# Attention chunks of 128 steps as two halves of 64 on quarters of TensorE, in a kernel with two dense layers

## The chip, the cores and the metric

The kernel runs on one core of a Trainium2 chip. The metric is the device time of one execution in microseconds (us), the median over runs. TensorE is called PE, VectorE DVE, ScalarE ACT, GpSimd POOL, and SyncE, whose queue issues all DMAs here, SP.

## What is computed

A gated linear attention (an mLSTM cell, with 4 batches, 8 heads, 768 steps and head size 40) is followed by two feed-forward layers of 3072 tokens x 320, with 2048 hidden units each.

```
for t in range(S):
    m_new = maximum(f[t] + m, i[t])
    f_stab, i_stab = exp(f[t] + m - m_new), exp(i[t] - m_new)
    C = f_stab * C + i_stab * outer(v[t], k[t])        # 40 x 40 state per head
    n = f_stab * n + i_stab * k[t]
    y[t] = sigmoid(o[t]) * (C @ q[t]) / maximum(abs(n @ q[t]), 1)
h = x @ w_in;  g = where(h >= 1, h, where(h <= -1, 0, (h + 1)**2 / 4));  x = g @ w_out
h = x @ w_in2; g = maximum(h, 0)**2;                   out = g @ w_out2
```

## The kernel before

**Attention.** The 768 steps of a batch are cut into 6 chunks of L = 128, which makes 24 chunks; they run step-major (the first chunk of each of the 4 batches, then the second ones). `attention` makes one chunk out of these steps on PE: `scores` (L618, 8 matmuls, one per head, on two 64-row halves of the array), `outer` (L653, 3 matmuls of 3 heads each, the chunk's contribution to the state), `read0` and `read1` (L690, 3 matmuls that read the state C of the previous chunk, and L694, 8 matmuls of weighted scores with v). All are fp32. The 128x128 decay matrix of each head comes from a scan along time on DVE (`decay`, L587, two of 512 elements for a chunk); its input is a row of gate factors that must stand on all 128 partitions. For the first 4 chunks PE spreads it (`spread`, L582), for the 20 others a DMA does (`fb`). `ab`, the decay from the chunk's start, is loaded for the 20 others too, and scales q (`q_in`, L639) and the old state (`update`, L667). `mask` (L673) keeps the blocks of the 3-head products that belong to one head. The ninth head is padding.

**Dense layers.** A chunk's 128 outputs are transposed (L767, or a DMA through DRAM), split into a high and a low half, and gathered in blocks of 3 chunks (layer one, 8 blocks) or 4 (layer two, 6 blocks). `dense` makes, for one block and one of 16 slices of hidden units, `mm1` (L828, 8 matmuls), an activation on ACT, DVE and POOL, and `mm2` (L888, 3 matmuls per chunk of the block). A weight slice arrives as float64 in a DMA of 704 KB (`wraw`) and is converted on ACT and DVE (L339 to L380) and split (L321, then L393, or for the slices of `PLO` on PE and ACT: `sub`, L428 and L429, and `put`).

**Order.** Nothing is issued as written: each step gets a rank (a due time plus the tables `MOVE` and `SHIFT_OF`), an engine and a cost, and `Plan.order` plays the list through and writes down each engine's order. Every engine then runs its own order strictly. Where the plan has nothing for PE, it puts idle matmuls of zeros (`idle`, L968, 400 of them), all in the first 63 us. Tiles come from pools with the numbers of buffers in `bufs`.

Of the kernel before, what the change touches and what calls it, by code (L numbers as in the profile page):

```python
# [13 lines left out]
U16 = mybir.dt.uint16  # L14
# [5 lines left out]
R = B * HP  # L20
L = 128
# [10 lines left out]
CST = 4 * L + 3 * E + 2  # L32

# [5 lines left out]
class Plan:  # L39
# [6 lines left out]
    TABLE = {"sig": "sigmoid", "a1": "exp", "a2": "exp", "a3": "exp"}  # L46
# [8 lines left out]
    def add(self, eng, rank, dur, fn, need=(), make=()):  # L55
# [5 lines left out]
        if self.group:  # L61
            kind, i = self.group
            rank += SHIFT_OF.get(kind, {}).get(fn.__name__, 0) + (MOVE[kind][i] if kind in MOVE else 0)
        self.tags.append(self.group)
        self.steps.append((eng, rank, fn, tuple(need), tuple(make)))

    def order(self):
# [49 lines left out]
        port, table = 0.0, None  # L117
        while len(out) < n:
# [41 lines left out]
def pool(n):  # L160
# [10 lines left out]
SPR = 4  # L171
# [6 lines left out]
EARLY = 1  # L178
QB = 1
GATE = -14  # L180
MOVE = {
# [8 lines left out]
}  # L190
SHIFT_OF = {
    "g": {"v1": -37.86, "v1f": 3.09, "v1i": 6.32, "a2": -19.57, "a3": 5.93, "p1": 92.77, "d1": 39.25,
        "tp": -0.65, "cp": 4.15, "a1": 24.16, "p2": 22.67, "v2": -89.15, "d2": -66.11},
    "w": {"load": 0.92, "a_move": 46.15, "v_clamp": 0.63, "a_tail": 26.69, "v_sign16": 0.71, "v_join": 0.16,
        "a_hi": 9.08, "v_lo": -1.71, "lo": -3.28, "sub": 40.36, "put": 19.14},
    "x": {"ld_qk": 5.06, "ld_vko": 0.42, "spread": 0.06, "decay": 0.65, "last": -81.57, "weigh": 1.85,
        "scores": -0.79, "v_in": -9.46, "sig": -40.49, "k_in": 4.18, "outer": -0.01, "update": -19.59,
        "read0": -0.49, "read1": -25.45, "norm_a": 0.11, "norm_b": -14.27, "norm_c": -9.8, "again": -32.29,
        "tr": 0.35, "hi": -27.45, "lo": -15.74, "ld_f": -3.57, "ld_q": 3.84, "ld_a": 33.49, "q_in": 9.92,
        "mask": 13.98, "turn": -23.51, "store": 14.75, "load": -1.24},  # L200
    "y": {"load": 0.18, "hi": -1.5, "lo": 54.98},
    "d": {"mm1": 0.62, "relu": 12.79, "square": 5.59, "gate": -1.83, "hi": 21.06, "lo": 6.71, "mm2": 3.97,
        "keep": 9.14, "evac": -16.97, "turn": -21.93, "store": -2.59},
}
# [17 lines left out]
def kernel(  # L222
# [14 lines left out]
        wraw=RAWB, wt=3, qk=2, vko=2, fb=1, qh=QB, ab=QB, d0=DB, d1=DB,  # L237
        ws=2, vt=2, qt=2, kt=2, sg=2, xn=2, rc=2, cx=1, C=5, xTh=XTB, xTl=XTB, pa=PAB, r=3, g0=3, g1=3, o=2, x2=2,
# [16 lines left out]
    csb = const.tile([128, CST], F32, name="csb")  # L255
# [282 lines left out]
    def attention(n, at, spr, early=0, bounce=False):  # L538
# [158 lines left out]
        def read0():  # L697
            read(0)
# [394 lines left out]
```

## Time and profile before

| | us |
|---|---|
| median of 3 runs (857.73 to 862.39) | 858.11 |
| the profiled execution | 861.52 |
| its span, first to last instruction | 859.7 |
| PE busy | 849.5 (99%) |
| DVE, ACT, POOL busy | 440.3, 449.7, 364.5 |
| DMA: 81.41 MB, the 16 engines' share | 33.2% |

Busy time of PE counts overlapping matmuls once, and a matmul's shown duration has its latency in it: what a step costs PE is read from start to start. An fp32 matmul of the program stands in the trace as two records.

### The profile page before, as it was taken

The numbers are of one execution on the slowest core, as the hardware profiler recorded it, in microseconds if no ns is written. First come the engines' busy times: TensorE is split into PE (matmuls) and PEld (weight loads), VectorE is DVE, ScalarE is ACT, GpSimd is POOL, SyncE is SP. The second block draws the span as 40 slices with busy tenths as digits, with TensorE's granted clock in tenths as the row PEclk, the third lists the DMA queues.
The fourth block names the chain that finished last, engine by engine and source line by source line (L and its number), as shares of the span: only waits on it lengthen the run. The fifth ranks groups of instructions, "written<-read, shape, count | busy, mean of one in ns | idle before, by whom it ended". The sixth has DMA issues, their size and how long they took to land.

```text
span 859.7 us, 14945 instructions
## 1 busy us (share of the span) xinstructions
PE 849.5 (99%) x5619; PEld 801.4 (93%) x5619; DVE 440.3 (51%) x758; ACT 449.7 (52%) x877; POOL 364.5 (42%) x349
## 2 busy tenths in 40 slices
PE   9998999999999999999999999999999999999998
PEld 8897999999999999999999999999999999999997
DVE  4998788987878734555224768721221111111111
ACT  5655566865545464444678866644333443533332
POOL 3221343032323435646565665645443533633332
PEclk9998899999999999999999999999999999999999
DMA  7767545455646533453231234101110100100000
GB/s 232 209 202 231 163 129 174 158 150 151 168 119 149 163 80 106 123 144 76 68 74 49 100 88 117 41 1 38 50 50 1 29 31 1 59 0 1 32 1 31
DMA packets 116957, 81.41 MB, mean 95 GB/s; under 512 B 57348, under 2 KB 105768, under 8 KB 116884
## 3 DMA queue, kind: packets, MB, share of 16 engines
q1 hardware_dynamic: 116884, 80.45, 33.2%
q8 instruction: 44, 0.72, 0.4%
q14 instruction: 29, 0.24, 0.1%
HBM read 69.90 MB, written 10.52 MB: 94 GB/s over the span
## 4 chain that ended last, share of the span: by engine, by line
PE 88%; DVE 4%; DMA 4%; ACT 2%; issue 1%; SPq 1%; POOL 0%; ACTq 0%; DVEq 0%; POOLq 0%
PE h L828 39%; PE acc L888 33%; PE v L888 5%; PE v L694 4%; DMA wraw<-in_wts_dram 2%; PE s L618 2%; PE v L690 2%; PE acc L968 1%; PE v L653 1%; DVE d L587 1%; DMA ab<-a 1%; DMA x<-xn 0%; DMA fb<-f 0%; DVE r L846 0%; DVE wt L380 0%
## 5 line engine op out<-in xcount | busy, mean ns | idle before, releaser
L860 POOL TENSOR_TENSOR xTh<-xTl,xTh 128x512 fp32r<-128x512 f32 x96 | 125.5, 1308 | 177.7 <-ACT xTh L321 177.7
L888 PE MATMUL acc<-w,g 128*128 128x320 f32 x1152 | 196.8, 313 | 0.7 <-ACT w L321 0.7
L848 DVE TENSOR_TENSOR xTl<-xTl,h 128x512 f32<-128x512 f32 x96 | 66.0, 687 | 233.3 <-ACT xTl L835 233.2
L888 PEld LDWEIGHTS acc<-w,g 128*128 128x128 f32 x1152 | 176.2, 188 | 2.5 <-ACT w L321 1.2
L828 PE MATMUL h<-xTh,w 128*128 128x384 f32 x640 | 177.9, 343 | 0.6 <-DVE r L846 0.4
L888 PE MATMUL acc<-w,xTh 128*128 128x320 f32 x864 | 143.3, 309 | 0.0
L888 PEld LDWEIGHTS acc<-w,xTh 128*128 128x128 f32 x864 | 134.6, 188 | 8.1
L828 PE MATMUL h<-qk,w 128*128 128x512 f32 x384 | 135.7, 394 | 0.0
L828 PE MATMUL h<-xTl,w 128*128 128x384 f32 x384 | 130.2, 339 | 0.0
L828 PEld LDWEIGHTS h<-xTh,w 128*128 128x128 f32 x640 | 118.1, 190 | 2.4 <-DVE r L846 0.9
L833 ACT ACTIVATE r<-h,half 128x384 f32<-128x384 f32 x128 | 74.0, 578 | 85.4 <-PE h L828 73.8
L846 DVE SCALAR_TENSOR_TENSOR r<-r,h 128x384 f32<-128x384 f32 x128 | 70.2, 549 | 93.1 <-ACT r L839 88.2
L835 ACT ACTIVATE xTl<-h 128x512 f32<-128x512 f32 x96 | 57.4, 598 | 108.8 <-PE h L828 107.6
L321 ACT ACTIVATE xTh<-xTl 128x512 fp32r<-128x512 f32 x96 | 60.7, 632 | 81.3 <-PE v L888 78.4
L860 POOL TENSOR_TENSOR g<-r,g 128x384 fp32r<-128x384 f32 x64 | 66.6, 1044 | 58.9 <-ACT g L321 54.8
L321 ACT ACTIVATE g<-r 128x384 fp32r<-128x384 f32 x128 | 66.4, 520 | 38.2 <-PE acc L888 35.5
L828 PEld LDWEIGHTS h<-qk,w 128*128 128x128 f32 x384 | 72.2, 188 | 12.5
L828 PE MATMUL h<-vko,w 128*128 128x512 f32 x192 | 75.6, 394 | 0.0
L828 PEld LDWEIGHTS h<-xTl,w 128*128 128x128 f32 x384 | 73.1, 190 | 0.0
L839 ACT ACTIVATE r<-r 128x384 f32<-128x384 f32 x128 | 66.9, 522 | 2.7
L828 PE MATMUL h<-d,w 128*128 128x512 f32 x192 | 60.3, 395 | 0.0
L639 POOL TENSOR_TENSOR qt<-qh,ab 120x384 f32<-120x384 f32 x20 | 23.0, 1150 | 86.6 <-DMA ab<-a 52.9
(103 smaller groups left out, 1142.1 us busy)
## 6 DMA issues: line engine op xcount, KB each, us to landing
wraw<-in_wts_dram SPq DMA_DIRECT2D x32, 704.0 KB
vko<-in_vko_dram SPq DMA_DIRECT2D x24, 524.5 KB
fb<-f SPq DMA_DIRECT2D x20, 512.0 KB
qk<-in_qk_dram SPq DMA_DIRECT2D x48, 160.0 KB
qh<-in_qh_dram SPq DMA_DIRECT2D x20, 180.0 KB
ab<-a SPq DMA_DIRECT2D x60, 60.0 KB
out_dram<-o SPq DMA_DIRECT2D x20, 160.0 KB
x<-x SPq DMA_DIRECT2D x24, 128.0 KB
```

Source lines behind the costliest of these rows:

```text
L321: nc.scalar.activation(out=out, in_=in_, func=ACTF.Copy)
L618: nc.tensor.matmul(out=z["s", a][:, h], lhsT=z["qk"][r, 0, h], rhs=z["qk"][r, 1, h], start=True, stop=True)
L639: engine[e].tensor_mul(out=z["qt"], in0=z["qh"], in1=z["ab"])
L694: nc.tensor.matmul(out=z["y"][:, E * h:E * (h + 1)], lhsT=z["d", a][:, h - 4 * a], rhs=z["vt"][:, h], start=(h == 0 and c == 0), stop=True ...
L828: nc.tensor.matmul(out=h, lhsT=a, rhs=b, start=(i == 0), stop=(i == 7))
L833: nc.scalar.activation(out=r, in_=z["h"], func=ACTF.Relu, scale=0.5, bias=half)
L835: nc.scalar.activation(out=r, in_=z["h"], func=ACTF.Relu)
L839: nc.scalar.activation(out=z["r"], in_=z["r"], func=ACTF.Square)
L846: nc.vector.scalar_tensor_tensor(out=r, in0=r, scalar=1.0, in1=z["h"], op0=ALU.min, op1=ALU.max)
L848: nc.vector.tensor_mul(out=r, in0=r, in1=z["h"])
L860: engine[e].tensor_sub(out=z["g1"], in0=z["r"], in1=z["g0"].bitcast(F32))
L888: nc.tensor.matmul(out=acc[k][:, 0:DM], lhsT=a, rhs=b, start=(f == f0 and i == 0), stop=(f == f1 - 1 and i == 2))
```

## The change

A chunk becomes two halves of U = 64 steps. `scores` makes the two 64x64 triangles' blocks of each head, and, in the same step, each half's contribution to the state, on all four 64x64 quarters of the array (row halves by operand partitions, column halves by output partitions). The state is kept for 8 heads as [104, 4, 41] (4 heads on partitions 0 to 39, 4 on 64 to 103), so no mask is needed, and there are two a chunk: `Ca` after the first half, `Cb` after the second. Each half reads the state in front of it: `cross` and half of `read0` take the states, the rest of `read0` and `read1` the weighted scores; these use two quarters on a diagonal at a time. Matmuls of different row halves add into the same place, so a copy on ACT (`after`) stands between `cross` and `read0`.

The first four chunks take their decays from sums of log gates on PE (`rise`, `sums`, `sumsa`) and exponentials on ACT (`grow`, `growa`), not from a scan; triangular masks for this are made on POOL (`masks`). For the other 20, `fb` and the scan are half as long, `qh` is not loaded (q comes from `qk`), and `ab` has two buffers, not one. Also: the weights' sign bit is put in by another DVE operation (`v_top` for `v_sign16`); 6 weight slices, not 3, take the way over PE (`PLO`); idle matmuls are 280; and the plan has new tables and a table for single steps.

```
-        plan.add(T, at - 4.5, 1.1, scores, [("qk", n)], [("s", (n, 0)), ("s", (n, 1))])
...
+        def scores():
+            z["s"] = [new("s", [128, 512]) for a in range(2)]
+            for h in range(4):
+                for u in sub:
+                    for a in range(2):
+                        nc.tensor.matmul(out=z["s"][a][u, U * h:U * h + U], lhsT=z["qk"][row[a], 0, h, u],
+                                         rhs=z["qk"][row[a], 1, h, u], start=True, stop=True)
+            kt = z["kt"].rearrange("p h e -> p (h e)")
+            for h in range(4):
+                for a, m in ((0, U), (1, D)):
+                    for u in range(1 + more):
+                        i = 4 * a + h
+                        nc.tensor.matmul(out=z["s"][u][U * a:U * a + m, 256 + E * h:256 + E * h + E],
+                                         lhsT=kt[sub[u], D * i:D * i + m], rhs=z["vt"][sub[u], i], start=True, stop=True)
...
+        def inter(u, a, h, start=False):
+            put(u, 4 * a + h, z["qt"][row[a], h, sub[u]], state(u)[row[a], h], start)
+        def intra(u, h, start=False):
+            put(u, h, z["d"][sub[u], h], z["vt"][sub[u], h], start)
+        def cross():
+            z["y"] = new(xy, [128, 512])
+            for h in range(4):
                 if c:
+                    inter(0, 1, h, h == 0)
+                inter(1, 0, h, h == 0)
+        def after():
+            nc.scalar.activation(out=new("tiny", [128, E])[U:128], in_=z["y"][U:128, 3 * E:4 * E], func=ACTF.Copy)
+        def read0():
+            for h in range(4):
+                if c:
+                    inter(0, 0, h)
+                inter(1, 1, h)
+            for h in range(4):
+                intra(0, h, c == 0 and h == 0)
+                intra(1, h)
+        def read1():
+            for h in range(4, H):
+                intra(0, h)
+                intra(1, h)
...
+        def rise(e):
+            z["up"] = t = new("d1", [128, H, U])
...
+                for h in range(H):
+                    nc.scalar.activation(out=t[:, h], in_=low["upto"], func=ACTF.Copy, scale=col[:, h:h + 1])
...
+        def sums():
+            z["fb"] = t = new(fx, [128, H, U])
+            for u in sub:
+                nc.tensor.matmul(out=t[u].rearrange("p h t -> p (h t)"), lhsT=low["past"][u],
+                                 rhs=z["up"][u].rearrange("p h t -> p (h t)"), start=True, stop=False)
...
+        def grow():
+            d = z["d"] = new("d0", [128, H, U])
+            nc.scalar.activation(out=d, in_=z["fb"], func=ACTF.Exp)
...
-EARLY = 1
-QB = 1
+EARLY = 4
+QB, CA, CB = 2, 3, 5
-FILL, FMM, FDUR = 200, 2, 0.14
+FILL = 140
-PLO = (5, 6, 7)
+PLO = (2, 3, 4, 5, 6, 7)
```

The order on PE where the first `mm1` stands, before (the end of the fourth chunk's `read1`, two idle matmuls ahead of it; `x2` and `acc2` are the idle matmuls' tiles):

```order
L694 MATMUL v_924<-vt_559,d0_758 128x41 x4
L968 LDWEIGHTS x2_151
L968 MATMUL acc2_153<-x2_151 128x160
L968 LDWEIGHTS x2_151
L968 MATMUL acc2_153<-x2_151 128x160
L694 MATMUL v_924<-vt_559,d1_781 128x41 x4
L828 MATMUL h_939<-xTh_556,w0_891 128x384
L828 MATMUL h_939<-xTl_561,w0_891 128x384
```

and in the change (the end of the fourth chunk's `scores`, the first `mm1`, a `sub`, the fourth chunk's `cross`, the second `mm1`):

```order
L739 MATMUL s_963<-vt_706,kt_755 40x41
L739 MATMUL s_964<-vt_706,kt_755 40x41
L946 MATMUL h_999<-xTh_646,w0_774 128x384
L946 MATMUL h_999<-xTl_666,w0_774 128x384
L946 MATMUL h_999<-xTh_646,w0_774 128x384 x2
L946 MATMUL h_999<-xTl_666,w0_774 128x384
L946 MATMUL h_999<-xTh_646,w0_774 128x384 x2
L946 MATMUL h_999<-xTl_666,w0_774 128x384
L470 MATMUL acc2_175<-wt_749,ident_81 128x352
L471 MATMUL acc2_175<-w2_951,nident_83 128x352
L783 MATMUL v_1028<-Ca_1015,qt_821 64x41 x4
L946 MATMUL h_1035<-xTh_646,w1_710 128x384
```

Ahead of the first `mm1` stand 384 idle matmuls, 8 `spread`s, 4 `scores`, 4 `outer`s, 4 pairs of reads and 2 `sub`s before; in the change it is 280 idle matmuls, 4 `sums`, 4 `sumsa`, 4 `scores`, 3 sets of reads and 1 `sub`. Behind it stand 16 idle matmuls and 4 `sub`s before, none and 11 in the change.

PE at a chunk's reads among dense work, before:

```order
L690 MATMUL v_1736<-C_1060,qt_1624 128x123 x3
L694 MATMUL v_1736<-vt_1476,d0_1449 128x41 x4
L888 MATMUL acc0_1651<-w2_760,g0_1629 128x320 x2
L888 MATMUL acc0_1651<-w2_760,g1_1663 128x320
L694 MATMUL v_1736<-vt_1476,d1_1497 128x41 x4
L888 MATMUL acc1_1659<-w2_760,g0_1629 128x320 x2
```

and in the change (the last matmuls of an `mm1` that stands between `cross` and `read0`, `read0`'s states and its scores, the next `mm1`, behind which `read1` comes; `Ca` and `Cb` are the two states):

```order
L946 MATMUL h_1797<-xTh_1279,w2_951 128x384 x2
L946 MATMUL h_1797<-xTl_1297,w2_951 128x384
L783 MATMUL v_1780<-Cb_1051,qt_1751 64x41
L783 MATMUL v_1780<-Ca_1771,qt_1751 64x41
L783 MATMUL v_1780<-Cb_1051,qt_1751 64x41
L783 MATMUL v_1780<-Ca_1771,qt_1751 64x41
L783 MATMUL v_1780<-Cb_1051,qt_1751 64x41
L783 MATMUL v_1780<-Ca_1771,qt_1751 64x41
L783 MATMUL v_1780<-Cb_1051,qt_1751 64x41
L783 MATMUL v_1780<-Ca_1771,qt_1751 64x41
L783 MATMUL v_1780<-vt_1676,d0_1480 64x41 x8
L946 MATMUL h_1840<-xTh_1279,w3_1011 128x384
```

A chunk's 11 + 11 fp32 matmuls of 128 or 120 columns became 32 + 32 of 64 or fewer, in four separate steps; from the first `mm1` on, the change has 608 in `scores` and 664 in the reads, in 82 stretches between full-array work.

## Rows read from the trace of the kernel before

**Rows 1.** The page, part 2: 40 equal slices, tenths busy, and tenths of granted clock.
```profile
PE   9998999999999999999999999999999999999998
...
PEclk9998899999999999999999999999999999999999
```

**Rows 2.** Busy time by stretch, us (instructions); then granted clock, DMA share, GB/s.
```profile
0.00:58.52 58.52, 56.23 (x621) 52.26 (x622) 44.68 (x74) 31.61 (x56) 15.15 (x20) 1.00 0.72 220
58.52:98.16 39.64, 35.56 (x230) 31.46 (x230) 30.22 (x54) 23.48 (x48) 11.07 (x11) 0.87 0.65 190
98.16:505.00 406.84, 406.44 (x2825) 400.64 (x2825) 264.53 (x492) 245.30 (x506) 179.80 (x180) 1.00 0.46 124
505.00:859.70 354.70, 351.23 (x1949) 317.05 (x1947) 100.83 (x141) 149.26 (x269) 158.44 (x139) 1.00 0.10 29
```

**Rows 3.** Timeline of PE in the saturated stretch: start, duration of the group, line, matmul records.
```profile
247.00 0.83 PE L690 MATMUL v<-C,qt 120*128 120x123 f32 x6
247.67 0.99 PE L694 MATMUL v<-vt,d 128*128 128x41 f32 x8
248.49 0.68 PE L888 MATMUL acc<-w,g 128*128 128x320 f32 x3
...
250.78 0.34 PE L828 MATMUL h<-xTh,w 128*128 128x384 f32 x1
...
252.19 1.48 PE L888 MATMUL acc<-w,g 128*128 128x320 f32 x9
253.60 1.16 PE L618 MATMUL s<-qk 40*128 40x128 f32 x16
254.69 0.44 PE L828 MATMUL h<-xTh,w 128*128 128x384 f32 x1
...
256.18 1.48 PE L888 MATMUL acc<-w,g 128*128 128x320 f32 x9
...
274.13 0.80 PE L653 MATMUL v<-vt,kt 128*120 128x123 f32 x6
...
276.09 0.33 PE L828 MATMUL h<-xTh,w 128*128 128x384 f32 x1
...
300.50 1.48 PE L888 MATMUL acc<-w,g 128*128 128x320 f32 x9
301.82 0.34 PE L828 MATMUL h<-xTh,w 128*128 128x384 f32 x1
...
303.21 1.48 PE L888 MATMUL acc<-w,g 128*128 128x320 f32 x9
```

**Rows 4.** Timeline of PE in the first 110 us.
```profile
1.29 9.04 PE L968 MATMUL acc<-x 128*128 128x160 bf16 x96 [1.29 <-DVE x L962]
...
11.10 1.15 PE L582 MATMUL h<-w,csb 36*128 36x128 f32 x8
12.18 0.31 PE L968 MATMUL acc<-x 128*128 128x160 bf16 x2
...
58.52 0.42 PE L828 MATMUL h<-xTh,w 128*128 128x384 f32 x1
...
69.73 0.75 PE L428 MATMUL acc<-wt,csb 128*128 128x352 f32 x2
70.06 0.59 PE L429 MATMUL acc<-w,nident 128*128 128x352 f32 x1
70.58 1.19 PE L618 MATMUL s<-qk 40*128 40x128 f32 x16
```

**Rows 5.** Groups of instructions by line and form: busy us, mean ns, idle before.
```profile
L587 DVE TENSOR_TENSOR_SCAN d<-fb,csb 128x512 f32<-128x512 f32 x40 | 51.0, 1280 | 9.4 <-PE v L694 8.9 <-DMA fb<-f 0.3
...
L968 PE MATMUL acc<-x 128*128 128x160 bf16 x400 | 33.8, 242 | 2.3 <-DVE x L962 1.3 <-ACT w L321 1.0
...
L739 ACT ACTIVATE xn<-xn 128x64 f32<-128x64 f32 x9 | 2.2, 244 | 0.5 <-DVE xn L723 0.5
```

**Rows 6.** The chain of waits in order of time, a piece: start, us, what.
```profile
74.39 5.38 DMA ab<-a
```

More of the change, by code (lines that the diff above doesn't have):

```diff
@@ L116, in order @@
         out = []
[L117 removed]
+        port, table = 0.0, "exp"
         while len(out) < n:
@@ L177 @@
 RAWB, DB = 3, 2
-EARLY = 1
-QB = 1
+EARLY = 4
+QB, CA, CB = 2, 3, 5
 GATE = -14
 MOVE = {
[8 rows of a table removed]
[6 rows of a table added]
 }
 SHIFT_OF = {
[L192 to L203, printed above, removed]
-}
@@ L205 @@
-FILL, FMM, FDUR = 200, 2, 0.14
+    "g": {"v1": 41.34, "v1f": 33.46, "v1i": -68.6, "masks": -68.95, "ft": -85.46, "fc": 23.57, "a3": 15.92,
+        "tp": -5.91, "cp": -0.45, "a2": -24.43, "p1": -33.39, "a1": 9.77, "p2": 37.31, "v2": 14.08,
+        "d1": -37.42, "d2": 13.4},
+    "w": {"load": 12.88, "a_move": 3.08, "v_clamp": -0.6, "a_tail": -2.4, "v_top": -10.71, "v_join": 8.44,
+        "a_hi": 7.18, "v_lo": 3.0, "lo": 8.23, "sub": -44.12, "put": 17.4},
+    "x": {"ld_qk": 9.96, "ld_vko": 4.17, "rise": -67.88, "sums": 13.61, "grow": -3.83, "sumsa": -17.97,
+        "growa": 1.3, "last": 9.63, "v_in": 28.51, "k_in": -25.42, "sig": 20.97, "q_in": 14.57,
+        "scores": 0.73, "update": -12.22, "scale": 16.24, "weigh0": -4.14, "weigh1": -53.01, "cross": -28.86,
+        "after": -36.49, "read0": -3.85, "read1": -17.99, "norm_a": -4.3, "norm_b": -14.46, "norm_c": -58.53,
+        "again": -8.4, "tr": -4.23, "hi": -8.78, "lo": -0.67, "ld_f": -1.42, "ld_a": 6.96, "decay": 22.69,
+        "turn": 52.31, "store": 16.87, "load": -16.23},
@@ L542, in attention @@
         z = t_["z", n] = {}
+        sub = [slice(U * u, U * u + U) for u in range(2)]
+        row = [slice(U * a, U * a + D) for a in range(2)]
         def ld_qk():
[L545 to L547 removed]
+            z["qk"] = new("qk", [G, 2, 4, L])
+            for a, w in ((0, U), (1, D)):
+                nc.sync.dma_start(out=z["qk"][U * a:U * a + w], in_=qk[n][0:w, :, 4 * a:4 * a + 4])
         def ld_vko():
@@ new lines, in sums @@
+        def sums():
[4 more added lines that the diff above has]
+            for u in sub:
+                nc.tensor.matmul(out=t[u], lhsT=low["upto16"][u],
+                                 rhs=low["veto"][u].rearrange("p (o t) -> p o t", o=1).to_broadcast([U, H, U]),
+                                 start=False, stop=True)
@@ L697, in read0, with q_in @@
-        def read0():
-            read(0)
-        def read1():
-            read(1)
-        plan.add(T, at - 1, 0.9 + (0.67 if c else 0), read0,
-                 [("d0", n, 1), ("vt", n)] + ([("qt", n), ("C", n - 1)] if c else []), [(xy, ("y", n))])
-        plan.add(T, at - 0.9, 0.9, read1, [("d1", n, 1), ("vt", n), (xy, ("y", n))], [(xy, ("y", n), 1)])
+        w = slice(0, L) if c else sub[1]
+        def q_in(e):
+            z["qt"] = new("qt", [G, 4, L])
+            engine[e].tensor_mul(out=z["qt"][:, :, w], in0=z["qk"][:, 1, :, w], in1=z["ab"][:, :, w])
@@ L954, in cst_rest @@
     def cst_rest():
-        nc.sync.dma_start(out=csb[:, L:CST], in_=cst[:, L:CST])
+        for u in range(2):
+            s = slice(U * u, U * u + U)
+            nc.sync.dma_start(out=eyes[s], in_=cst[s, s].rearrange("p (o t) -> p o t", o=1).to_broadcast([U, 8, U]))
     plan.add(Y, -40, 0.8, cst_rest, make=[("cst", 0)])
```

451 lines of the change are left out of this document (257 added, 194 removed), and 14 rows, old and new, of the table MOVE.

## Prediction, made before the change was run

> **What bounds the kernel now.** I read the page's slices first: PE is busy nine tenths or more of nearly every slice, and its granted clock is full almost throughout [rows 1]. Busy time hides what PE is busy with, so next come the stretches [rows 2]. From 98 us to the end PE idles only 0.4 us of 406.8 and then some at the very end: there every microsecond of PE work is a microsecond of the result, and DVE (264.5 of 406.8), ACT and POOL have room. The first 98 us are different: up to 58.5 us, where the first `mm1` starts [rows 4], PE's time is the attention of the first chunks and idle matmuls, and from there to 98.2 us PE idles 4.1 us (39.64 less 35.56) and runs at a mean granted clock of 0.87, which is another 0.13 x 39.64 = 5.2 us: 9.3 us of stalls [rows 2]. DVE is the busiest other engine there (44.7 of 58.5, 30.2 of 39.6). One piece of the chain shows such a stall: a DMA of `ab` of 5.38 us at 74.4 us [rows 6]. So two things count: PE work behind the first `mm1`, and when that `mm1` can start. The dense work itself (1.39 us for an `mm1` of block size 3, 1.32 us for its nine `mm2` matmuls [rows 3]) is untouched.
>
> **The price of attention on PE now.** From start to start [rows 3]: `scores` with the `mm1` and nine `mm2` matmuls around it takes 256.18 - 252.19 = 3.99, less 2.71 is 1.28; its own 16 records take 1.09, so 0.19 goes to entering and leaving. `outer` costs 276.09 - 274.13 - 1.32 = 0.64. The reads cost 250.78 - 247.00 - 1.32 = 2.46 (0.67 for the states; nine `mm2` matmuls lie among the rest). Behind the first `mm1` stand 20 `scores`, 16 `outer`s and 20 sets of reads: 25.6 + 10.2 + 49.2 = 85.0 us.
>
> **The price of a record.** With all of the array, a record takes 0.67 / 6 = 0.111 us at 123 moving columns and 0.82 / 8 = 0.1025 at 41 [rows 3]: three times the columns change little, so the 128 stationary columns set it. On one 64-row half alone, L582's 8 records take 12.18 - 11.10 = 1.08 us, 0.135 each [rows 4]; on two halves in turn, L618's take 1.09 / 16 = 0.068 [rows 3]. So two tiles run fully beside each other. No row shows quarters. Halving L618's columns gives 0.034 for two quarters in turn and, if four run as freely as two, 0.017 for four. Halving 0.1025 for the columns and again for each doubling of tiles gives 0.0256 and 0.0128. I take the middle, 0.030 and 0.015, as I know no reason to prefer an end, and keep both.
>
> **What the change costs there.** The 608 matmuls of `scores` (four quarters) are 1216 records x 0.015 = 18.2 us; the 664 of the reads (two) are 1328 x 0.030 = 39.8. Each of the 82 stretches is entered and left; between the 0.08 of the reads before (2.46 less 0.67 and twice 0.82, for two entries) and L618's 0.19 I take 0.19, as L618 also changes the array's division: 15.6. At 0.08 it would be 9.0 less. Sum 73.6 against 85.0: **-11.4 us**. The Trainium skill's page "TensorEngine Tiling (Array Packing)", section "Key Properties", says that a change of tiling mode drains TensorE. That speaks against this change, which has four such steps in a chunk where there was one. The 0.19 beside the 0.08 agrees with it; by that rule the 9.0 us are not to be had, and without it they would be.
>
> **Weight slices and idle matmuls behind the first `mm1`.** A `sub` costs 70.58 - 69.73 = 0.85 us of PE [rows 4]; seven more are **+6.0**. Sixteen idle matmuls at 0.08 go: **-1.3**.
>
> **The first `mm1`.** An idle matmul costs 9.04 / 96 at the start [rows 4] and (33.8 - 9.04) / 304 = 0.081 later [rows 5]. Before: 384 of them 32.5, 8 `spread`s 8.6, 4 `scores` 5.1, 4 `outer`s 2.6, 4 reads without states (2.46 - 0.67) 7.2, 2 `sub`s 1.7, idle 2.3: 60.0 without the transposes, which stay as they are, where the trace has 58.5, so this recipe is a little high. In the change: 280 idle matmuls 24.0; 4 `sums`, whose 512 columns I price like a `spread` (4 x 128 columns) plus 0.2, 5.2; 4 `sumsa` of 16 records at 0.030, 1.9; 4 `scores` of 64 at 0.015, 3.8; 3 sets of reads of 48 at 0.030, 4.3; 16 stretches 3.0; one `sub` 0.9; idle as before 2.3: 45.4, which is 14.6 less. Against this stands ACT. It was busy 31.6 of 58.5 us [rows 2]; `rise` for two chunks is 16 copies of 64 columns at 0.244 [rows 5] = 3.9 us, and eight exponentials of 256 or 512 columns, 2 us or more by the same row, and more switches of its table come on top, in a ramp 15 us shorter: ACT goes from half busy to most of the time. I allow 3 us: **-11.6**, the first `mm1` at 47 us. DVE is relieved: the 8 scans of the first four chunks go, and the others halve (48 scans of about 1.28 us [rows 5] become 20). POOL's masks stand ahead of its first gate step and need only be done when `sums` starts; if late they delay `rise`, which the 3 us cover.
>
> **The stalls between the first `mm1` and 98 us.** `ab` of the first chunks no longer comes by DMA, has two buffers, and the loads of a chunk with state fall (`qh` gone, `fb` halved); DVE has less. But 11 `sub`s now wait there for ACT and ACT for them. Of 9.3 us I keep 6: **-3.3**.
>
> **At nothing.** The sign step stays one DVE operation over 704 elements; scale and update of a second state, POOL's larger `q_in`, `after` on ACT (24 copies of about 0.24 us [rows 5]) all lie beside PE in the saturated stretch, where each engine is busy 65% or less [rows 2]. `after` adds a wait: `read0` and all dense work behind it stop PE if ACT is late. Mostly an `mm1` of 1.39 us stands between, against 0.24 for the copy; in the ramp it is sometimes only `mm2` matmuls and a transpose, which the 6 us of stalls cover. Without that cover each chunk would pay the copy and about as much for what ACT has in hand, 0.5 us, 10 in all.
>
> **Sum.** -11.6 - 11.4 + 6.0 - 1.3 - 3.3 = -21.6 us. It is made against the profiled execution (861.5 us, its span 859.7), which was 3.4 above the median; the median of 858.1 less 21.6 is **836.5 us** (-2.5%).
>
> **The rivals.**
> - *Quarters shrink as far as rows allow* (0.0128 and 0.0256, entering at 0.08, stalls 3): 1472 records of `scores` in all x 0.0022, 1536 others x 0.0044, 98 stretches x 0.11 and 3 are 23.8 less: 813. For it: L582 and L618 show perfect overlap of two tiles. Chance 0.16.
> - *A floor for a record*: four quarters go no faster than two, 0.0256: 1472 x 0.0106 = 15.6 more, 852. The Trainium skill's page "TensorE: Matmul & The Clock Gate" (section "Wait — 56ns, not 53.3ns?") states a floor from start to start of about 25 ns, and of about 62 ns where the sequencer's microcode handles matmuls. No row here is under 0.068 us, so no run yet shows which holds. Chance 0.11.
> - *The ramp gives nothing*: ACT or the weight loads (0.72 of the DMA share already [rows 2]) hold the first `mm1` at 58 us, or PE's waits bring the clock down as between 58 and 98 us: 11.6 + 3.3 back, 851. Chance 0.12.
> - *Slower: records that do not halve.* L582's 0.135 is 0.0325 more than the 0.1025 of a full array. If that part belongs to a record whatever its size, a quarter's is 0.051 + 0.0325 = 0.084, or 0.042 with two in turn and 0.021 with four: 1472 x 0.006 + 1536 x 0.012 = 27.3 more, 864. It decides from 21.6 / 3008 records = 7 ns over my prices on. At its end quarters would not run beside each other more than L618's halves, every record staying at 0.068: the change would not do what it says, and cost over 100 us. Chance 0.09.
>
> **How the numbers follow.** The forecast has 0.52; its own range is 822 to 849. The range of 812 to 858 takes in the fast case and the floor and leaves out about one in seven, mostly slow. A measurement here can tell 0.5% (4.3 us) from no change: faster are the forecast, the fast case and most of the floor and the ramp rival (0.09 each), 0.86; within 0.5% the rest of those two, 0.05; slower 0.09.
>
> **What would show it.** Start to start, `scores` with states near 0.96 us and a set of reads near 1.9 plus entries; the first `mm1` at 44 to 50 us; PE busy throughout afterwards; no scan on DVE for the first four chunks. Wrong: `scores` over 1.4 us, PE waiting at `read0` for `after`, or clock rows under 1.0 past 55 us.

## The result, and the profile after

| | before | after |
|---|---|---|
| median, us | 857.92 (856.82 to 862.39, 4 runs) | 847.93 (847.36 to 849.17, 4 runs) |
| the profiled execution | 861.52 | 847.36 |
| its span | 859.7 | 845.6 |
| first `mm1` starts | 58.52 [rows 4] | 49.34 |
| from there to PE's last matmul's end | 797.7 | 792.9 |
| PE, DVE, ACT, POOL busy | 849.5, 440.3, 449.7, 364.5 | 834.3, 395.3, 466.2, 378.5 |

The change saves 10.0 us in the median, a ratio of 0.9876 (95% interval 0.9839 to 0.9912). The time lies inside the forecast's own range (822 to 849 us), but the forecast gain was 21.6 us. (The 858.11 of the kernel before is the median of three of these four runs.)

The page, part 2 (busy tenths and granted clock by slice) answers to [rows 1]: PE is still busy throughout.

```profile
PE   8989999999999999999999999999999999999998
...
PEclk9999999999999999999999999999999999999999
```

Busy time by stretch, in the columns of [rows 2]. Between the first `mm1` and 98 us PE idles nothing and its clock is whole; the 9.3 us of stalls of the kernel before are gone. Before the first `mm1`, DMA is busier than it was (0.78) and ACT has 35.1 of 49.3 us.

```profile
0.00:49.34 49.34, 42.98 (x788) 35.33 (x788) 29.64 (x60) 35.12 (x71) 21.00 (x37) 1.00 0.78 221
49.34:98.16 48.82, 48.82 (x686) 42.19 (x683) 42.50 (x79) 37.85 (x83) 26.36 (x28) 1.00 0.67 205
98.16:505.00 406.84, 405.28 (x4138) 385.19 (x4137) 235.10 (x452) 253.22 (x515) 182.48 (x196) 1.00 0.41 109
505.00:845.60 340.60, 337.21 (x1875) 304.69 (x1873) 88.02 (x129) 140.03 (x255) 148.63 (x131) 1.00 0.10 31
```

The timeline of PE in the saturated stretch answers to [rows 3] (start, duration of the group, line, records). L732 and L739 are `scores` with the states (64 records), L783 the reads, L946 `mm1`, L1006 `mm2`.

```profile
303.95 1.49 PE L1006 MATMUL acc<-w,g 128*128 128x320 f32 x9
305.28 0.34 PE L946 MATMUL h<-xTh,w 128*128 128x384 f32 x1
...
306.67 1.05 PE L1006 MATMUL acc<-w,g 128*128 128x320 f32 x6
307.65 0.69 PE L732 MATMUL s<-qk 40*64 40x64 f32 x32
308.16 0.61 PE L739 MATMUL s<-vt,kt 64*64 64x41 f32 x32
308.71 0.44 PE L946 MATMUL h<-xTh,w 128*128 128x384 f32 x1
...
310.30 0.25 PE L783 MATMUL v<-Cb,qt 40*64 40x41 f32 x1
310.30 0.25 PE L783 MATMUL v<-Ca,qt 40*64 40x41 f32 x1
310.37 0.23 PE L783 MATMUL v<-Cb,qt 40*64 40x41 f32 x1
310.38 0.23 PE L783 MATMUL v<-Ca,qt 40*64 40x41 f32 x1
310.43 0.23 PE L783 MATMUL v<-Cb,qt 40*64 40x41 f32 x1
...
310.72 0.23 PE L783 MATMUL v<-Cb,qt 40*64 40x41 f32 x1
310.73 0.23 PE L783 MATMUL v<-Ca,qt 40*64 40x41 f32 x1
310.89 1.59 PE L1006 MATMUL acc<-w,g 128*128 128x320 f32 x9
312.32 0.34 PE L946 MATMUL h<-xTh,w 128*128 128x384 f32 x1
```

Two prices can be read here. **A record:** the `Cb` records, all on one quarter, start 0.0583 us apart ((310.72 - 310.37) / 6), and those of `Ca` run on the other quarter beside them, 7 ns behind. With two quarters that is 0.029 us a record, and with four 0.0146: the 64 records of `scores` take 308.71 - 307.65 = 1.06, of which the 16 on one quarter are 0.93. These are nearly the values that the prediction took (0.030 and 0.015). **A stretch:** this set of 16 records lasts 310.89 - 310.30 = 0.59 us, of which eight records on each quarter are 0.47, so 0.12 goes to its first and last record. The nine `mm2` behind it take 312.32 - 310.89 = 1.43, where nine among dense work take 305.28 - 303.95 = 1.33: 0.10 for leaving. The six ahead of `scores` take 307.65 - 306.67 = 0.98, where two thirds of 1.33 are 0.88: 0.10 for entering. A stretch on quarters thus costs 0.32 us besides its records; the prediction took 0.19. It is not this set alone: in after_third (the changed kernel in a further profile, below), between 100 and 400 us, a set costs 0.79 us if it has 16 records on two quarters (34 sets) and 1.25 if it has 32 on two (17 sets) or 64 on four (12 sets), with what the dense matmuls on either side take longer. Less the records, that is 0.32 each time.

In the ramp (the time up to the first `mm1`) three rows of PE are worth a look: two waits (for POOL's `qt`, and for `xn`, a copy on ACT), and the first `mm1`.

```profile
18.44 0.48 PE L783 MATMUL v<-Ca,qt 40*64 40x41 f32 x5 [1.73 <-POOL qt L718]
...
44.70 0.33 PE L884 MATMUL s<-ident,xn 128*128 128x128 f32 x1 [1.77 <-ACT xn L847]
...
49.34 0.44 PE L946 MATMUL h<-xTh,w 128*128 128x384 f32 x1
```

Ahead of that copy ACT itself stood 6.01 us at the load of a weight slice:

```profile
42.96 0.83 ACT L419 ACTIVATE wt<-wraw 128x704 f32<-128x704 f32 x1 [6.01 <-DMA wraw<-in_wts_dram]
...
44.40 0.24 ACT L847 ACTIVATE xn<-xn 128x64 f32<-128x64 f32 x1
```

### The profile page after: what moved, and what is told of

The parts are those of the page before. It is cut to its first block, busy times and chain, and to the rows that moved or that the text cites. A ratio compares the mean times of both kernels' runs of the same rounds, so it can differ in the third digit from the quotient of the medians.

```text
span 845.6 us, 18712 instructions
## 1 busy us (share of the span) xinstructions
PE 834.3 (99%) x7478; PEld 767.4 (91%) x7478; DVE 395.3 (47%) x718; ACT 466.2 (55%) x920; POOL 378.5 (45%) x392
## 4 chain that ended last, share of the span: by engine, by line
PE 92%; DMA 4%; ACT 2%; SPq 1%; issue 0%; DVE 0%; ACTq 0%
PE h L946 42%; PE acc L1006 35%; PE v L783 5%; PE v L1006 5%; DMA wraw<-in_wts_dram 3%; PE s L732 2%; PE s L739 1%; PE acc L470 1%; DMA x<-xn 0%; SPq L612 0%; ACT L711 0%; ACT wraw L425 0%; PE s L884 0%; PE acc L1088 0%; PE acc L471 0%
## 5 line engine op out<-in xcount | busy, mean ns | idle before, releaser
L1006 PE MATMUL acc<-w,g 128*128 128x320 f32 x1152 | 199.9, 314 | 0.0
L1006 PEld LDWEIGHTS acc<-w,g 128*128 128x128 f32 x1152 | 176.1, 188 | 3.4 <-DVE g L978 0.2
L946 PE MATMUL h<-xTh,w 128*128 128x384 f32 x640 | 177.0, 341 | 0.2 <-DVE r L964 0.2
L1006 PE MATMUL acc<-w,xTh 128*128 128x320 f32 x864 | 142.9, 309 | 0.0
L1006 PEld LDWEIGHTS acc<-w,xTh 128*128 128x128 f32 x864 | 134.6, 188 | 8.2
L946 PE MATMUL h<-qk,w 128*128 128x512 f32 x384 | 135.7, 394 | 0.0
L946 PE MATMUL h<-xTl,w 128*128 128x384 f32 x384 | 129.6, 337 | 0.0
L951 ACT ACTIVATE r<-h,half 128x384 f32<-128x384 f32 x128 | 74.2, 580 | 85.2 <-PE h L946 65.6
L953 ACT ACTIVATE xTl<-h 128x512 f32<-128x512 f32 x96 | 57.4, 598 | 113.6 <-PE h L946 113.5
L946 PEld LDWEIGHTS h<-xTh,w 128*128 128x128 f32 x640 | 116.9, 188 | 1.5 <-DVE r L964 0.3
L946 PEld LDWEIGHTS h<-qk,w 128*128 128x128 f32 x384 | 72.1, 188 | 12.8
L946 PE MATMUL h<-vko,w 128*128 128x512 f32 x192 | 75.6, 394 | 0.0
L946 PEld LDWEIGHTS h<-xTl,w 128*128 128x128 f32 x384 | 72.3, 188 | 0.0
L946 PE MATMUL h<-d,w 128*128 128x512 f32 x192 | 60.4, 396 | 0.0
L1006 PE MATMUL v<-w,xTh 128*128 128x320 f32 x288 | 57.7, 309 | 0.0
```

Source lines behind the costliest of these rows:

```text
L946: nc.tensor.matmul(out=h, lhsT=a, rhs=b, start=(i == 0), stop=(i == 7))
L951: nc.scalar.activation(out=r, in_=z["h"], func=ACTF.Relu, scale=0.5, bias=half)
L953: nc.scalar.activation(out=r, in_=z["h"], func=ACTF.Relu)
L1006: nc.tensor.matmul(out=acc[k][:, 0:DM], lhsT=a, rhs=b, start=(f == f0 and i == 0), stop=(f == f1 - 1 and i == 2))
```

## The experiments

Kernels of one group ran on one chip. The kernel before has a median of 859.3 to 860.1 us on the chips of groups 1 to 3 and of 856.0 on that of group 4, so ratios to it are what compares across groups.

### Group 1: the baseline, the quarters, the ramp

**before_again** changes nothing.

> The kernel before, unchanged, profiled a second time. Its first profiled execution took 861.5 us, 3.6 above its median, and lost 9.6 us between its first mm1 (58.5 us) and 98 us: 4.4 us of waits of PE and 5.2 us by a granted clock of 0.87. Theory: those stalls differ from execution to execution, so an execution near the median shows 3 to 4 us less of them (5.5 to 6.5 us), the first mm1 again at 58 to 59 us, and the rest of the trace the same. Rival: the stalls are fixed by the order of the work; an execution near the median has its 9.6 us of stalls too, and the 3.6 us lie elsewhere (an earlier first mm1, or shorter dense work).

It took 858.72 us (one execution). Its first two stretches, in the columns of [rows 2]:

```profile
0.00:59.23 59.23, 56.82 (x622) 52.85 (x622) 44.86 (x74) 31.55 (x56) 15.94 (x20) 1.00 0.70 218
59.23:98.16 38.93, 35.34 (x249) 31.25 (x249) 32.93 (x61) 24.93 (x52) 14.02 (x14) 0.96 0.72 210
```

PE waits 3.8 us from the first `mm1` on, nearly as long as in the first profile (4.4), but the clock costs 0.04 x 38.93 = 1.6 us and not 5.2. From the first `mm1` to PE's last end it is 794.2 us against 797.7, and the clock is nearly all of that: some 3.6 us of the stalls that the prediction saw to be won are not there in an execution near the median. The theory held.

**pairs** puts the records of one step in another order.

```
-            for h in range(4):
-                for u in sub:
-                    for a in range(2):
+            for x in range(2):
+                for h in range(4):
+                    for a in range(2):
+                        u = sub[a ^ x]
...
-            for h in range(4):
-                for a, m in ((0, U), (1, D)):
-                    for u in range(1 + more):
+            for a, m in ((0, U), (1, D)):
+                for u in range(1 + more):
+                    for h in range(4):
```

> The changed kernel with the same 64 records in each scores step, in another order: those of the triangles alternate between two quarters of the array at a time, those of the states run on one quarter until it is done, then on the next. Theory (what counts is how many quarters are at work side by side; a quarter alone takes 0.066 to 0.074 us for a record): the triangles' 32 records go from 0.51 us to 1.06 to 1.18, the states' 32 from 0.55 to 2.1 to 2.4, a step from 1.06 to between 3.2 and 3.5, and with some 19 such steps behind the first mm1 the kernel takes 885 to 895 us. Rival (the order does not matter; the reads cost 0.037 us a record for what they are, sums into PSUM with 41 stationary... columns or 40 rows): scores stays at 1.06 to 1.2 and the time at 848.

It took 860.71 us (one execution). The timeline of PE around one such step (L733 triangles, L740 states):

```profile
66.55 0.80 PE L733 MATMUL s<-qk 40*64 40x64 f32 x26
67.14 0.25 PE L740 MATMUL s<-vt,kt 64*64 64x41 f32 x1
...
67.33 1.01 PE L740 MATMUL s<-vt,kt 64*64 64x41 f32 x29
68.27 0.86 PE L470 MATMUL acc<-wt,ident 128*128 128x352 f32 x2
```

The step takes 68.27 - 66.55 = 1.72 us, not 1.06, and not 3.2 either; 0.66 us in 16 such steps and 0.23 in the four of the last chunks behind the first `mm1` are 11.5 us, about what this is slower than the changed kernel as it is (850.1 and 849.4 us in groups 2 and 3). So both theories were wrong as they stood: order matters, but PE does not finish one set of quarters before it starts the next. In the trace's single records the second pair of quarters begins 0.30 us after the first, which has three of its eight records on each quarter still to come; on every quarter with 64 stationary columns the records are 0.058 us apart whatever runs beside it, and with the 40 columns of the second state group 0.035 to 0.04.

**banks** gives the reads of the states a second PSUM bank and all four quarters.

```
-            z["y"] = new(xy, [128, 512])
+            z["y"] = [new(xy, [128, 512])]
+            if bounce:
+                z["y"].insert(0, z["s"][0][:, 256:256 + 4 * E])
             for h in range(4):
                 if c:
                     inter(0, 1, h, h == 0)
+                if bounce:
+                    inter(1, 1, h, h == 0)
                 inter(1, 0, h, h == 0)
+                if bounce:
+                    inter(0, 0, h, h == 0)
...
```

> The changed kernel; for the last 15 of the 24 chunks the four groups of reads of the states run on all four quarters in rotation in one step, which needs a second PSUM bank for the sums (columns of the scores tile that are free by then); the reads of the triangles stay on two quarters. Each such chunk has two small operations of DVE more in norm_a and one in norm_c. Theory (quarters side by side set the price): a chunk's reads go from 2.24 us (0.59 + 1.06 + 0.59) to 1.7 (0.53 + 0.59 + 0.59), which is 15 x 0.53 = 8 us; the order of the work shifts a little with the waits of the plan, so 838 to 842 us. Rival (sums into PSUM cost a record 0.035 us however many quarters work): reads stay at 2.2 and the time at 847 to 850.

Median 848.91 us, ratio 0.9865 (0.9831 to 0.9900). The timeline of PE in one set:

```profile
316.47 0.25 PE L784 MATMUL v<-Cb,qt 40*64 40x41 f32 x1
316.48 0.25 PE L784 MATMUL v<-Ca,qt 40*64 40x41 f32 x1
316.49 0.25 PE L784 MATMUL s<-Ca,qt 40*64 40x41 f32 x1
316.49 0.25 PE L784 MATMUL s<-Cb,qt 40*64 40x41 f32 x1
...
317.08 1.14 PE L1023 MATMUL acc<-w,g 128*128 128x320 f32 x6
```

Twice the records (32) take 317.08 - 316.47 = 0.61 us, and the middle set, now 16 records, falls from 1.06 to 0.59: four quarters run beside each other as freely as two, sums into PSUM or not. The 6.8 us that 15 chunks save on PE did not reach the time: PE now waited 4.5 us for DVE and 0.6 for POOL near 410 us, and the first `mm1` came at 52.9 us.

**unblock** moves six steps in the order of the first 46 us; this list is applied to the planner's result.

```
...
+LATER = [("v_join", ("w", 2), "v_clamp", ("w", 2)), ("a_move", ("w", 3), "a_hi", ("w", 2)),
+         ("a_tail", ("w", 3), "a_move", ("w", 3)), ("sig", ("x", 3), "a_tail", ("w", 3)),
+         ("decay", ("x", 4), "lo", ("x", 1)), ("v_top", ("w", 3), "decay", ("x", 4))]
```

> The changed kernel with six steps moved in the order of the first 46 us: on ACT the two steps on the fourth weight slice, which wait for its load until 42.9 us, go behind the copies that block 0 needs, and a sigmoid behind them; on DVE the join of the third slice goes ahead of the scan and of the step that waits for the fourth slice. Nothing else moves. Theory (the first mm1 is at 49.3 us because ACT stood 6.0 us at a load while the third chunk's outputs waited behind it): the first mm1 starts at 46 to 46.8 us and the kernel takes 844.5 to 846. Rival A (weight loads bound what follows too): the first mm1 is as early, but PE waits for weights between 46 and 98 us, and the time stays at 847 to 849. Rival B (PE's own attention and idle matmuls set the start): the first mm1 stays at 49.

Median 850.85 us, ratio 0.9896 (0.9866 to 0.9926), the first `mm1` at 49.17. Its granted clock was 0.53 between 20 and 25 us and 0.78 between 25 and 30, where the first profile of the changed kernel has 1.00, so the expected 46 us could not be seen. Against two profiles of the changed kernel as it is with such a dip of the clock (52.2 and 52.4 us, below) the first `mm1` is 3 us earlier, and PE then waits 2.6 us for ACT's weights, as rival A has it. Group 4 repeats it without the dip.

### Group 2: banks alone, joined sets, subs

**after_again** changes nothing.

> The changed kernel, unchanged, on the chip of the next three and profiled a second time. Theory: the granted clock in the first 50 us differs from execution to execution (1.00 in the first profile; 0.90 to 0.93 in those of the two variants whose first 25 us are the same): a dip to half clock near 20 to 30 us moves the first mm1 from 49.3 to as late as 52.9 us, so a second profile with a dip shows the first mm1 at 50 to 53 us and 847 to 850 us. Rival: the dip belongs to the variants; the first mm1 is at 49.3 us again and the time at 847.4 to 848.

Median 850.10 us, ratio 0.9906 (0.9880 to 0.9932). The profile has the dip (0.50 between 20 and 25 us) and its first `mm1` at 52.37 us. The dip belongs to the changed kernel, and the first profile was the lucky one: its mean granted clock is 1.00, and 0.995 or 0.996 in the three other executions of the result.

**ybanks** writes the two halves' sums to two banks; of the reads themselves it changes only which half of a pair comes first in `read0`, and the first set waits for two things more.

```
...
-            nc.tensor.matmul(out=z["y"][sub[u], E * h:E * h + E], lhsT=lhsT, rhs=rhs,
+            nc.tensor.matmul(out=z["y"][u][sub[u], E * h:E * h + E], lhsT=lhsT, rhs=rhs,
...
+            if bounce:
+                z["y"][1] = z["s"][0]
...
```

> The changed kernel; in the last 15 of the 24 chunks the two halves of a chunk's reads write two PSUM banks in turn (64 partitions of one and 64 of the other) instead of one. The reads keep their records, quarters, order and the two quarters at a time; norm_a has two small operations of DVE more, norm_c one. Theory A (quarters: what counts is how many work side by side, two here): a set of reads stays at 0.59 + 1.06 + 0.59 us, the time at 847 to 851. Theory B (banks: a record that follows another into the same PSUM bank takes 0.030 to 0.037 us, and writing two banks in turn halves that; the scores write two banks, the reads one): the sets become 0.28 to 0.32 + 0.53 to 0.6 + 0.28 to 0.32, 1.1 us less for each of 15 chunks or 16 us in all, of which waits on DVE as in the variant with four quarters (5 us there) may give some back: 832 to 840 us.

Median 855.86 us, ratio 0.9956 (0.9934 to 0.9978). One set of PE's timeline (`v` is one bank, `s` the other):

```profile
301.53 0.25 PE L783 MATMUL v<-vt,d 64*64 64x41 f32 x1
301.54 0.25 PE L783 MATMUL s<-vt,d 64*64 64x41 f32 x1
...
302.12 1.59 PE L1018 MATMUL acc<-w,g 128*128 128x320 f32 x9
```

It takes 0.59 us as ever: the bank does not set the price, and theory B fell. The 5.8 us over the changed kernel as it is, on this chip, are for the most part waits of PE for DVE, ACT and POOL (5.0 us between 409 and 422 us); behind them the granted clock is lower too (0.90 from 410 to 425 us, another 1.5 us).

**merge** makes one step of the last two sets of reads of a chunk and lets the planner order everything anew.

```
...
-        plan.add(T, at - 1, 1.1, read0, used + [D0 + (1,), YK + (1,), ("vt", n)], [YK + (2,)])
-        plan.add(T, at - 0.9, 0.46, read1, [D0 + (2,), YK + (2,), ("vt", n)], [YK + (3,)])
+        plan.add(T, at - 1, 1.6, read0, used + [D0 + (2,), YK + (1,), ("vt", n)], [YK + (3,)])
```

> The changed kernel with the last set of reads of a chunk put into the one before it, which then waits for both halves of the weights: about 20 stretches on quarters fewer behind the first mm1. Theory (entering and leaving a stretch costs 0.10 us each way, on the dense matmul before it and on the one after it): 20 x 0.20 = 4 us less, 843.5 to 845 us. Rival (the longer step waits for DVE): PE shows waits of the reads on weigh of DVE and the time stays at 847 to 850.

Median 854.03 us, ratio 0.9940 (0.9915 to 0.9965). The joined set takes 1.52 us instead of 1.06 + 0.59, as the theory wants, but the new order put the first `mm1` at 57.4 us and left many small waits. It tested the planner and not the price.

**sub3** takes half of the low parts from PE.

```
-PLO = (2, 3, 4, 5, 6, 7)
+PLO = (5, 6, 7)
```

> The changed kernel with the low parts of weight slices 2 to 4 taken by DVE or POOL, as in the kernel before, and only those of slices 5 to 7 by PE: 6 of the 12 subs go. Theory (each sub costs PE 0.84 us, nothing waits for DVE): the first mm1 comes no later and 5 subs behind it save 4.2 us: 843 to 845. Rival (DVE, 82% busy between 40 and 98 us, is late with the low parts): PE waits on DVE or POOL there by 3 to 8 us and the time is 847 to 852.

Median 880.27 us, ratio 1.0274 (1.0238 to 1.0309). The subs' share of PE fell from 9.2 to 5.5 us, and this is what PE waited for (engine, line, releaser; us in all, times, longest):

```profile
PE v L783 <- DVE sg L840: 10.8, 4, 4.3
PE h L946 <- DVE r L964: 4.9, 5, 1.7
PE h L946 <- DVE w L447: 2.6, 1, 2.6
```

The rival was right and too small: DVE was late up to 260 us, and in its wake PE's clock fell to a mean of 0.91 from 98 to 300 us. The 6 us for seven more subs are well spent.

### Group 3: the price of a stretch, and the dip

**after_third** changes nothing.

> The changed kernel, unchanged, beside the next three on one chip. Both theories: 847 to 851 us, with the first mm1 at 49.3 us if the granted clock holds through the first 50 us and at 51.5 to 53 us if it dips near 20 to 30 us.

Median 849.39 us, ratio 0.9877 (0.9856 to 0.9899); the profiled execution took 848.52, with the first `mm1` at 52.20. Its first two stretches, in the columns of [rows 2]:

```profile
0.00:52.20 52.20, 46.84 (x787) 39.19 (x787) 29.29 (x60) 35.23 (x71) 20.53 (x37) 0.93 0.76 208
52.20:98.16 45.96, 45.96 (x667) 39.33 (x664) 40.10 (x73) 35.74 (x78) 23.84 (x26) 1.00 0.70 211
```

**join1** keeps the planner's order and moves one step of PE in 20 chunks; a stable sort then puts every step behind what it needs.

```
...
+        for k in range(4, NCH):
+            r0, r1 = name["read0", ("x", k)], name["read1", ("x", k)]
+            late += [(r0, j) for j in pe[pe.index(r0) + 1:pe.index(r1)]]
...
```

> The changed kernel; behind the first chunks the middle set of reads of each of 20 chunks is issued later on PE, directly ahead of the last set. No other step changes its place, and the number of records stays. 82 stretches on quarters behind the first mm1 become 62. Theory (a stretch costs 0.32 us besides its records at 0.0583 us on each quarter: 0.10 on the dense matmul before it, 0.12 in its own first and last record, 0.10 on the dense matmul behind it): 20 x 0.32 = 6.4 us less than the unchanged kernel between the first mm1 and the end; a joined set takes 1.52 us from start to start, where the two took 1.06 + 0.59. Rival A (the price of entering is 0.19 us, as the prediction had it): 3.8 us less. Rival B (what comes later on PE makes DVE late): the 6.4 us come back as waits of PE.

Median 845.28 us, ratio 0.9834 (0.9812 to 0.9856). A joined set in the timeline of PE:

```profile
313.62 0.25 PE L811 MATMUL v<-Cb,qt 40*64 40x41 f32 x1
...
314.11 1.11 PE L811 MATMUL v<-vt,d 64*64 64x41 f32 x32
315.15 1.15 PE L1034 MATMUL acc<-w,g 128*128 128x320 f32 x6
```

315.15 - 313.62 = 1.53 us for 24 records on each of two quarters (1.40) and one pair of ends. From the first `mm1` to PE's last end it is 785.6 us, of which 0.4 wait, against 791.2 and no wait in after_third: 6.0 us for 20 stretches, 0.30 each. Less its waits, this stretch of the trace is 791.2 or 791.3 us in all four profiles of the changed kernel's order of PE (after, after_again, after_third, warm), so 6.0 can be told from 3.8. Rival A (3.8) and rival B (nothing) fell.

**warm** adds 20 idle matmuls.

```
+            if n == 0:
+                for _ in range(20):
+                    nc.tensor.matmul(out=t_["idle_ps"][:, WH // 2:], lhsT=t_["idle"][:, 0:128],
+                                     rhs=t_["idle"][:, WH // 2:], start=True, stop=True)
             z["y"] = new(xy, [128, 512])
```

> The changed kernel with 20 idle matmuls more (1.6 us) just ahead of the first reads, where PE waits 1.7 us for POOL near 17 us. Theory (the dip of the granted clock to half near 20 to 30 us follows that wait): no dip, the granted clock at 1.00 in every stretch up to 50 us, the first mm1 at 49.3 us or before, and 2 to 3 us less than executions with a dip. Rival (the dip has another cause, or PE has slack there): the granted clock between 20 and 30 us is 0.5 to 0.8 again, or the first mm1 is as late without it.

Median 845.46 us, ratio 0.9846 (0.9823 to 0.9870), the first `mm1` at 48.75. Busy time by stretch (columns of [rows 2]) from 15 to 30 us, first of after_third, then of warm:

```profile
15.00:20.00 5.00, 2.90 (x104) 2.50 (x103) 1.96 (x6) 2.34 (x6) 1.86 (x3) 1.00 1.00 344
20.00:25.00 5.00, 5.00 (x124) 4.63 (x121) 2.82 (x5) 4.88 (x7) 0.64 (x2) 0.51 0.42 144
25.00:30.00 5.00, 5.00 (x54) 3.75 (x55) 4.07 (x11) 3.95 (x7) 4.14 (x5) 0.80 0.31 88
```

```profile
15.00:20.00 5.00, 5.00 (x142) 4.60 (x140) 2.36 (x8) 3.34 (x8) 2.52 (x4) 1.00 0.96 320
20.00:25.00 5.00, 5.00 (x138) 4.44 (x138) 3.92 (x9) 4.91 (x7) 1.75 (x3) 1.00 0.59 193
25.00:30.00 5.00, 4.77 (x69) 2.96 (x65) 2.46 (x4) 4.92 (x8) 2.76 (x3) 1.00 0.46 135
```

With 2.10 us of waiting in 15 to 20 us PE gets half its clock behind it (1.2 instead of 2.4 GHz); with work in that gap the clock holds. The start gains 52.20 - 48.75 = 3.4 us, and the medians differ by 3.9.

**join1w** has both edits.

> Both edits together. Theory: both gains, 838 to 842 us. Rivals: as for each alone.

Median 840.86 us, ratio 0.9779 (0.9758 to 0.9800): the two gains add (8.5 us, of 4.1 and 3.9), and this version beats both kernels. Less its waits, the stretch from the first `mm1` on is 785.0 us, against 791.3 in warm: 20 stretches again save 0.31 each.

### Group 4: what was left open

**unblockw** has the moves of unblock and the idle matmuls of warm.

> The changed kernel with the six moved steps of the first 46 us (the two ACT steps on the fourth weight slice behind the copies that block 0 needs) and with the 20 idle matmuls that keep PE going near 17 us, so that the granted clock does not hide what the moves do. Beside it stands the variant with the idle matmuls alone: first mm1 at 48.75 us, 845.5 us. Theory (ACT standing at the load of the fourth slice sets the first mm1): the first mm1 at 46 to 46.8 us, 843 to 844 us. Rival A (the weights of the next slices bound what follows): the first mm1 as early, then waits of PE for ACT's weights of 2 us or more near 50 us, 845 to 848 us. Rival B (PE's own work sets it): the first mm1 stays at 48.7.

Median 847.60 us, ratio 0.9896 (0.9867 to 0.9926). Its timeline of PE:

```profile
46.02 0.44 PE L959 MATMUL h<-xTh,w 128*128 128x384 f32 x1
...
49.63 0.86 PE L479 MATMUL acc<-wt,ident 128*128 128x352 f32 x2 [1.95 <-ACT w L410]
...
55.95 1.52 PE L479 MATMUL acc<-wt,ident 128*128 128x352 f32 x2 [1.29 <-ACT w L410]
```

The first `mm1` is at 46.0 us, as the theory had it, and rival A takes back all of it and more (the ratio of warm alone is 0.9846): PE stands 3.2 us for the next weight slices, and its granted clock falls to a mean of 0.80 between 50 and 60 us. So what bounds PE once its start is earlier is the supply of weights through ACT; which part of that supply (the loads or ACT's own work) was not taken apart.

**bjw** has banks, join1 and warm together.

> Four quarters for the reads of the states in the last 15 chunks (0.45 us less in each: the first set stays at 0.6 us with twice the records, the middle one falls from 1.06 to 0.59), the two later sets joined in 20 chunks, and the 20 idle matmuls near 17 us, all in one kernel. Theory (prices add: 0.0583 us a record on each quarter with all quarters in parallel, 0.3 us a stretch): 15 x 0.45 = 6.8 us less PE work than the variant with the other two edits (840.9 us), of which the waits of PE for DVE near 410 us (4.5 us there when it was tried alone) give back up to 5: 834 to 839 us. Rival: the later sums in a second bank make DVE late more often: 841 or more.

Median 841.75 us, ratio 0.9828 (0.9800 to 0.9857). The work of attention on PE falls again (59.4 us of own time behind the first `mm1`, where join1w has 65.6), but PE waits for DVE as in banks:

```profile
PE h L995 <- DVE r L1013: 4.3, 2, 3.5
```

It also shows the dip (0.67 between 20 and 25 us) in spite of the idle matmuls; in the planner's new order PE waits 0.8 us for `qt` ahead of it. So prices add on PE, and the rival won the time: join1w stays the best.

## Why the prediction was wrong, term by term

I set the terms against a pair of executions near the medians, before_again (span 856.9) and after_third (846.7).

| term | predicted | measured |
|---|---|---|
| first `mm1` | -11.6 | -7.0 (59.23 to 52.20) |
| attention behind it | -11.4 | -2.4 |
| seven more subs | +6.0 | +5.9 (0.84 each) |
| idle matmuls | -1.3 | -1.1 |
| stalls | -3.3 | -5.4 (3.8 of waits and 1.6 of clock, to nothing) |
| sum | -21.6 | -10.0, and the spans differ by 10.2 |

The measured attention term is what the others leave of the 3.0 us by which the stretch behind the first `mm1` became shorter (794.2 to 791.2). By prices it is nearly the same: 1216 records x 0.0146 + 1328 x 0.0291 + 82 stretches x 0.32 = 17.8 + 38.6 + 26.2 = 82.6, against the 85.0 of the kernel before.

**The step that failed** is "I take 0.19" for entering and leaving a stretch. The records were priced right: what sets a record is its own quarter (0.0583 us at 64 stationary columns, about half of the 0.112 at which single records with 128 follow each other), and quarters do not slow each other. The stretch was 0.13 us too cheap, 82 times, which is 10.7 us. Records that cost 1.6 less than taken bring the attention term's miss to 9.0; the first `mm1` missed by 4.6, the small terms by 0.1, and the stalls gave 2.1 more than forecast: 11.6 in all.

The error was in the reading of [rows 3]: I took the 0.19 beside L618's own 1.09 us for the whole of entering and leaving, while 1.09 had more of it inside. Eight records on each half at 0.111, the price that the prediction itself read for 128 stationary and 123 moving columns, are 0.89, so about 0.39 of the 1.28 us were not records, and the rows showed it. The other bound was misread too: at 0.111 the 22 records of a chunk's reads are 2.44 of their 2.46 us, so those stretches, on the whole array, cost nothing to enter, and not 0.08. A price of 0.3 or more thus belonged to the steps that divide the array, and the change has only such steps.

Here the rule of the Trainium skill's page "TensorEngine Tiling (Array Packing)", section "Key Properties" (a change of tiling mode drains TensorE), was the one to weigh more. The traces agree with it: in the kernel before, the divided `scores` cost 0.39 us besides their records and the sets on the whole array nothing, and in the change a stretch costs about 0.3 us for going in and out, which join1 confirms (6.0 us for 20 stretches). The page gives no price.

**The first `mm1`** came 2.3 us later than forecast in the first profile and 5.2 in one near the median. The recipe of PE's work was not at fault; "idle as before 2.3" was, and a clock that it put at full speed. In the first profile PE stands 6.4 us ahead of its first `mm1` (49.34 less 42.98): 45.4 and the 4.1 more are 49.5. In after_third it stands 5.4 us (52.20 less 46.84) and loses some 3.5 by the clock between 20 and 30 us: 45.4 + 3.1 + 3.5 = 52.0. (The 1.5 us by which the recipe is high and the 2.1 that its 16 stretches lack nearly cancel.) Two things stand behind this: the wait of 1.7 to 2.1 us for POOL's `qt` near 17 us, behind which the clock dips in all profiles of this order but the first (warm wins 3.4 us of the start back), and ACT standing at a weight load ahead of `xn`. With ACT's and DVE's order changed (unblockw) PE is at its first `mm1` at 46.0 us, where the forecast has 47, but then the supply of weights bounds the next step. I had put 3 us on ACT's busy time; what counted was what ACT waited for.

**The stalls** went altogether, more than the 3.3 us allowed. But the profile that I summed against had 3.6 us more of them than an execution near the median, by its clock alone. To take that sum off the median was therefore wrong: against the median 5.4 us could be won and not 9.3. That all of it was won, where 6 were to stay, made up for this by luck, and the term came out 2.1 us better than forecast. Profile against profile the gain is 14.1 us, but there an execution that lost much by its clock stands against a lucky one.

**The rivals.** Slower by records that do not halve (864) named the wrong thing, since records halve, but the point that part of a stretch's time does not shrink with its size was the right one. Its 0.0325 us a record was misread in the same way: the single records of L582 start 0.112 us apart, and what is left of the 1.08 us lies at the ends of the stretch. The fast case (813) had records and stretches too cheap. The ramp rival (851) named the right causes, but 7.0 of the 11.6 us came all the same. The floor of a record did not show: records on different quarters start 7 ns apart (as those on L618's two halves did in the trace of the kernel before, where the prediction read only their mean of 0.068 us), below the 25 ns that the Trainium skill's page "TensorE: Matmul & The Clock Gate" (section "Wait — 56ns, not 53.3ns?") gives as the least from start to start; the measurement decides, at least for records on different tiles. `after`, which the prediction costed at nothing, made PE wait only 1.9 us in all of the first profile (0.6 in the ramp, 1.3 near 268 us) and not at all in after_third.

Most of the signs that the prediction named came as if it were right: `scores` took 1.06 us from start to start, the first `mm1` of the first profile stood at 49.3, and PE was busy with a whole clock behind it. None of them looked at the dense matmuls on either side of a stretch, where most of its price lies.

## What to carry to other kernels

Small matmuls on parts of the array are priced in two parts: the cadence of one tile times the records of the tile that has most, and a fixed price for each uninterrupted stretch. Take the second from whole stretches, by what the dense work on either side loses too, and then arrange the work for few stretches before arranging it for many tiles: putting two neighbouring sets together paid 4 us here. Take the difference between two profiles against a profile near the median, and before an engine is called the bound of a start-up, look at what it is waiting for.

## What the runs showed of the hardware that was not expected

- Records on the four quarters do not disturb each other: with 64 stationary columns each quarter keeps 0.0583 us from start to start whether one, two or four are at work (single records of after and pairs), and two quarters take 0.59 us a set whether they write one PSUM bank or two (ybanks). In `pairs` PE even started on a free quarter while records for a busy one were still to come.
- A stretch in another division of the array costs about 0.1 us on the dense matmul ahead of it, 0.1 on the one behind it and 0.12 in its own ends (after; 0.30 in all in join1). In the kernel before, sets of small records on the whole array cost nothing besides their 0.112 us a record, and the one step on two halves (L618) 0.39.
- A wait of PE of 1.0 to 2.1 us near 17 us was followed by about half the clock (0.50 to 0.53) between 20 and 25 us in the profiles of after_again, after_third, join1, unblock, banks, ybanks, merge and sub3, and not in the first profile, whose wait was 1.73 us; so the length of the wait alone does not decide. Idle matmuls in the gap kept the clock in warm, join1w and unblockw, and `pairs`, where PE hardly waits there (0.1 us), has a whole clock between 20 and 30 us too.
